# Column sums of V's weights moved from TensorE to VectorE, four raw blocks, and a re-paired set of first loads

## The chip, the cores and the metric

The kernel runs on one core of one Trainium2 chip. The metric is the device time of one execution in microseconds (us). A core has five engines with a program each: TensorE (PE in the profile, PEld for its weight loads), VectorE (DVE), ScalarE (ACT), GpSimd (POOL) and SyncE (SP). DMA transfers are issued from the queues of SP, ACT and POOL, which the profile calls SPq, ACTq and POOLq.

## The reference

```python
xn  = layernorm(x)                                  # x: 2048 x 512, no scale or shift
# A: local dilated attention, 32 heads of 16, window of 8 keys two rows apart
q, k, v = split(xn @ wqkv)                          # wqkv: 512 x 1536
o   = softmax(q . k[s - 2w], w = 0..7) weighted sum of v[s - 2w]
A   = o @ wo
# B: gated MLP
z   = gelu(xn @ w_in)                               # w_in: 512 x 1792, halves z1, z2
g   = w_sp @ layernorm(z2) + b_sp                   # w_sp: 2048 x 2048
B   = (z1 * g) @ w_out                              # w_out: 896 x 512
out = x + A + B
```

Everything is bfloat16 with float32 accumulation.

## The kernel before

The 2048 rows are handled as 16 blocks of 128 rows (index b), and as 4 waves of 512 rows (index j or tc). The program is not written in its final order. Each step is a task with an engine, inputs, outputs, an estimated duration and a priority. A planner (`Plan.schedule`) places the tasks in time by these estimates, gives out the eight PSUM banks, and so fixes the order of instructions on every engine and every DMA queue; the hardware then runs each engine's list strictly in that order and waits on semaphores. For the first microseconds part of the order is written by hand: lists of task names that must follow one another (`for names in (...)`), and a table `land` of the moments at which the planner is to believe the first loads landed.

The tasks that the change and the prediction touch, with their lines in the profile of before:

- Loads. `ldx0` (L541) and `ldx1` go out on ACT's queue; `ldwv0`, `ldwv1` (V's weights in two halves, L518), `ldx2`, the two halves `ldwin2a` (L524) and `ldwin2b` (L530) of z2's weights, `ldx3` to `ldx7` (L514), `ldq` and `ldk` (L536) and `ldx8` to `ldx15` go out on SP's queue, in this order.
- `ln_block(b)`: `bnst` and `bnag` take mean and variance on DVE (L599, L601), `vpe` adds epsilon (L609), POOL takes the power -1/2 (`rstd`, L611), DVE normalises (`norm`, L623). The normalised block is then turned, so that features lie on partitions: blocks 0 to 3 by four small PE matmuls (`xTr`, L579) and an ACT copy (`xTe`, L587), blocks 4 to 15 by a DMA transpose on SP's queue (`xTd`, L617).
- Raw blocks. V of blocks 0 and 1 does not wait for the normalisation. PE turns the raw x (`xTx`, L579), ACT copies it (`xTc`, L606), PE multiplies it with V's weights (`V0`, `V1`, L654), and the mean is taken out afterwards: `cs_0` and `cs_1` (L638) multiply a matrix of ones with V's weights, which puts minus the column sums on every partition (`cse`, L642), `fix0` and `fix1` (L660, DVE) add mean times column sum, and `Ve0`, `Ve1` (L663, ACT) scale by `rstd` and write the result. From block 2 on V is computed from the turned normalised block, and `Ve` only copies. POOL's queue writes every V block to DRAM (`Vw`, L668).
- PE's main work, in the order of the program: z2 = gelu(...) in blocks (`z2_b`, L766, eviction L774, squares L779), Q and K in pairs per wave (`Q0_0`, `K0_0`, ..., L677, eviction `QKe` L686), z1 (L812), the big product g with `w_sp` (L907), and the output blocks `outo_b` and `out_b` (L963, L972).
- DVE's main work: the products of Q and shifted K (`prod`, `padd`, L698 and L703), the softmax steps (L728 to L752), normalisation of z2 (`zn`, L798), the weighted sums of V per block (`pv`, `pva`, `pvb`, `pvc`, L935 to L941), the gating (`gb`, `u`, L918 and L921) and the last addition of every output block (`fin_b`, L978). `red0` and `red2` (L713) are small PE steps that sum the products over a head; `red2` stands in the middle of g and needs `padd3_3`, the last of the products.
- Output blocks use PSUM banks in turn: until block 5 they alternate between two banks, so `outo4` needs `fin2` and `outo9` needs `fin7`.

Of the kernel before, what the change touches and what calls it, by code (L numbers as in the profile page):

```python
# [36 lines left out]
class Plan:  # L37
# [85 lines left out]
    def schedule(self, dma_bw=300.0, xbar_bw=190.0, dma_lat=1300.0, dma_pre=400.0, issue=None, tol=40.0, land=None,  # L123
# [49 lines left out]
        while left:  # L173
            pick = None
            for e in ENGS:
                sc = []
                for t in cand[e]:
                    r = max(t.ready, free[e])
                    for b in t.banks:
                        if b.base is None:  # L180
                            p = place(b)
                            if p is None:
                                r = None
                                break
                            r = max(r, p[2])
# [31 lines left out]
            if t.dma is not None:  # L217
                iss = issue[e]
                t.eng_end = r + iss
# [4 lines left out]
                t.end = xe + dma_lat  # L224
# [114 lines left out]
def build_kernel(nc, A_x, A_wqkv, A_wo, B_x, B_w_in, B_w_sp, B_b_sp, B_w_out, out, report=False, emit=True):  # L339
# [11 lines left out]
    NXT = 4  # L351
    NWARM = 8
# [3 lines left out]
    vscr = nc.dram_tensor("vscr", (16 + S, 512), BF).ap()  # L356

# [13 lines left out]
    place(3584, w_in1=0, tg=0, On=2048, xcT=0, ncs=1024)  # L371
# [8 lines left out]
    off["xn"] = off["attn"]  # L380
    AR = top[0]
# [4 lines left out]
    for name, n in (("prime", 4), ("mx", 128), ("Zb", 256), ("Z", 128), ("maskt", 128), ("st6", NB * 6),  # L386
                    ("mv", NB * 2), ("vpe", NB), ("rstd", NB), ("s1", NB), ("s2", NB), ("m2", NB), ("msq", NB),
# [8 lines left out]
    with ExitStack() as es:  # L396
# [57 lines left out]
        R1(("wqk", 0), "wqk", 2048)  # L454
        R1(("wqk", 1), "wqk", 2048, 2048)
        for s_ in range(2):
            R1(("wv", s_), "wv", 1024, 1024 * s_)
# [8 lines left out]
        for hf in range(2):  # L466
            for b in range(2):
                R1(("xcT", b, hf), "xcT", 256, 512 * b + 256 * hf)
            R(("xnT", 0, hf), "sb", [(off["xnT"] + dc * S, off["xnT"] + dc * S + 128) for dc in (2 * hf, 2 * hf + 1)])
        R1("ncs", "ncs", 1024)  # L470
# [20 lines left out]
        def dma(eng, fn, nbytes, chan, reads=(), writes=(), name="", xbar=False, prio=0.0, after=()):  # L491
            return T(eng, fn, reads=reads, writes=writes, name=name, prio=prio, after=after,
                     dma=dict(chan=chan, nbytes=nbytes, xbar=xbar))
# [7 lines left out]
        ncs = A("ncs", 1024).bitcast(F32)  # L501
# [15 lines left out]
        def ld_wv(hf):  # L517
            dma("sp", lambda e: e.dma_start(AC(off["wv"] + 1024 * hf, [[512, 2], [1, 512]]),  # L518
                                            A_wqkv[256 * hf:256 * hf + 256, 1024:1536].rearrange("(c p) n -> p c n",
                                                                                               p=128)),  # L520
                256 * 512 * 2, ("wv", hf), writes=[("wv", hf)], name="ldwv%d" % hf)
# [13 lines left out]
        def ld_wqk(which, eng):  # L535
            dma(eng, lambda e: e.dma_start(  # L536
                AC(off["wqk"] + 2048 * which, [[512, 4], [1, 512]]),
                A_wqkv[:, 512 * which: 512 * which + 512].rearrange("(c p) n -> p c n", p=128)),
                512 * 512 * 2, ("wqk", which), writes=[("wqk", which)], name="ld%s" % ("qk"[which]))

        dma("act", lambda e: e.dma_start(A("xin", 512), x2[0:128, :]), 128 * 512 * 2, ("xin", 0),  # L541
            writes=[("xin0", 0), ("xin0", 1)], name="ldx0")
        ld_x(1, "act")
        ld_wv(0)
        ld_wv(1)
        ld_x(2, "sp")
        ld_win2a()
        ld_win2b()
        ld_x(3, "sp")
        ld_x(4, "sp")  # L550
        ld_x(5, "sp")
        ld_x(6, "sp")
        ld_x(7, "sp")
        ld_wqk(0, "sp")
        ld_wqk(1, "sp")

# [16 lines left out]
        def pe_tr(src, keys, name):  # L573
# [8 lines left out]
            T("pe", tr, reads=keys + ["ident"], writes=[bk], est=(430.0 if name == "xTx0" else 4 * c_mm(128)), name=name)  # L582
# [10 lines left out]
        def ln_block(b):  # L593
# [9 lines left out]
            if b < 2:  # L603
                bc = pe_tr(xin, xk, "xTx%d" % b)
                for hf in range(2):
                    T("act", (lambda hf: lambda a: a.activation(A("xcT", 256, 512 * b + 256 * hf), P(bc, 256, 256 * hf),  # L606
                                                                ACTF.Copy))(hf),
                      reads=[bc], writes=[("xcT", b, hf)], est=c_act(256), name="xTc%d_%d" % (b, hf), prio=-1)
# [23 lines left out]
        def colsum():  # L632
            bk = plan.bank("cs")
            for hf in range(2):
                def mm(t, hf=hf):
                    last = None
# [433 lines left out]
```

## Time and profile before

| | us |
|---|---|
| three executions | 236.80, 237.02, 237.28 |
| median | 237.02 |
| span of the profiled execution, first to last instruction | 236.1 |
| what lies around the span, against the median | 0.9 |
| PE busy in the span | 231.7 |
| DVE busy | 207.4 |
| ACT busy | 96.5 |
| POOL busy | 32.7 |
| granted TensorE clock, mean | 1.000 |

Busy time of an engine is the union of its instructions; a matmul is counted to the end of its drain, so a busy PE says that matmuls follow one another, not that each is at its peak. The start of one 128x512 matmul follows the one before by 0.216 us, that of a 128x448 one by 0.189 us, and four 128x128 ones take 0.224 us from the first start to the next group, although the profile's durations for them are 0.379, 0.352 and 0.219 us.

### The profile page before, as it was taken

Reading aid. Unit: us, or ns where it says so; the run is one execution under the profiler, and the core shown is the slowest. Engines: PE = TensorE matmul, PEld = TensorE weight load, DVE = VectorE, ACT = ScalarE, POOL = GpSimd, SP = SyncE. Lnnn points to the kernel's source line nnn. Section 1 sums busy time; section 2 is a strip of 40 time slices with the busy share of each in tenths; the row PEclk is TensorE's granted clock in tenths of the full one; section 3 lists DMA queues with packets and bytes.
Section 4 is the critical chain, followed back from the end, with each engine's and each line's share of the span. In section 5 each row is a group of like instructions: output and inputs, shape, how many; then the busy total and the mean of one; then the engine's idle time right before and its main releaser. Section 6 shows DMA issues by size and latency. Waiting matters only on the chain.

```text
span 236.1 us, 2974 instructions
## 1 busy us (share of the span) xinstructions
PE 231.7 (98%) x1114; PEld 109.1 (46%) x1135; DVE 207.4 (88%) x269; ACT 96.5 (41%) x145; POOL 32.7 (14%) x56
## 2 busy tenths in 40 slices
PE   8999999999999999999999999999999999999996
PEld 3455555555444444444444444444444444444443
DVE  3799899999998899999699998986989997999432
ACT  3598889888967895510120531111111111000000
POOL 2259650311733100000000000000000000000000
PEclk9999999999999999999999999999999999999999
DMA  7998969991048325430999999998995959936432
GB/s 211 352 283 163 243 146 217 195 202 44 22 165 260 92 85 69 104 118 0 226 347 252 225 266 180 200 304 187 346 258 175 261 161 303 193 95 181 135 96 69
DMA packets 82013, 43.86 MB, mean 186 GB/s; under 512 B 54336, under 2 KB 81360, under 8 KB 82000
## 3 DMA queue, kind: packets, MB, share of 16 engines
q1 hardware_dynamic: 80768, 41.27, 71.5%
q0 software_dynamic: 800, 2.11, 2.8%
q10 hardware_dynamic: 432, 0.30, 0.6%
q8 instruction: 9, 0.15, 0.3%
q14 instruction: 4, 0.03, 0.1%
HBM read 26.35 MB, written 4.21 MB: 129 GB/s over the span
## 4 chain that ended last, share of the span: by engine, by line
PE 94%; DMA 3%; SPq 1%; ACT 1%; issue 1%; DVE 0%
PE ps L907 41%; PE ps L677 12%; PE ps L972 10%; PE ps L812 10%; PE ps L766 9%; PE ps L963 6%; PE ps L654 5%; DMA arena<-in_B_w_in_dram 3%; PE ps L713 1%; ACT arena L774 0%; SPq L518 0%; ACT arena L587 0%; PE ps L579 0%; SPq L514 0%; SPq L524 0%
## 5 line engine op out<-in xcount | busy, mean ns | idle before, releaser
L907 PE MATMUL ps<-arena 128*128 128x512 bf16 x439 | 96.6, 379 | 0.5
L907 PEld LDWEIGHTS ps<-arena 128*128 128x128 bf16 x448 | 43.7, 98 | 53.1 <-issue 0.4
L915 ACT ACTIVATE arena<-ps 128x1024 bf16<-128x1024 f32 (+1 forms) x16 | 14.7, 917 | 78.0 <-PE ps L907 78.0
L698 DVE TENSOR_TENSOR arena<-arena 128x4096 bf16<-128x4096 bf16 x16 | 36.5, 2282 | 0.1
L935 DVE TENSOR_TENSOR arena<-arena 128x4096 bf16<-128x4096 bf16 x16 | 36.4, 2283 | 0.0
L938 DVE TENSOR_TENSOR arena<-arena 128x2048 bf16<-128x2048 bf16 (+1 forms) x32 | 29.9, 948 | 0.0
L677 PE MATMUL ps<-arena 128*128 128x512 bf16 x126 | 28.7, 379 | 0.1
L703 DVE TENSOR_TENSOR arena<-arena 128x4096 bf16<-128x4096 bf16 x12 | 27.4, 2287 | 0.1
L972 PE MATMUL ps<-arena 128*128 128x512 bf16 (+2 forms) x117 | 26.9, 366 | 0.1
L766 PE MATMUL ps<-arena 128*128 128x448 bf16 x128 | 26.0, 352 | 0.5 <-DMA arena<-in_B_w_in_dram 0.5
L812 PE MATMUL ps<-arena 128*128 128x512 bf16 x110 | 24.4, 379 | 0.1
L978 DVE TENSOR_TENSOR arena<-ps,arena 128x512 bf16<-128x512 f32 (+2 forms) x17 | 11.2, 658 | 11.7 <-PE ps L972 11.7
L677 PEld LDWEIGHTS ps<-arena 128*128 128x128 bf16 x128 | 14.5, 113 | 13.0
L766 PEld LDWEIGHTS ps<-arena 128*128 128x128 bf16 x128 | 12.3, 98 | 12.7 <-ACT arena L642 0.7
L686 ACT ACTIVATE arena<-ps 128x1024 bf16<-128x1024 f32 x16 | 16.3, 1021 | 4.4 <-PE ps L677 4.1
L972 PEld LDWEIGHTS ps<-arena 128*128 128x128 bf16 x119 | 11.4, 98 | 12.8
L812 PEld LDWEIGHTS ps<-arena 128*128 128x128 bf16 x112 | 10.9, 98 | 13.2 <-ACT arena L818 0.3
L963 PE MATMUL ps<-arena 128*128 128x512 bf16 (+2 forms) x66 | 16.5, 366 | 0.1
L774 ACT ACTIVATE arena<-ps 128x896 bf16<-128x896 f32 x16 | 14.6, 914 | 3.2 <-PE ps L766 3.1
L818 ACT ACTIVATE arena<-ps 128x1024 bf16<-128x1024 f32 (+1 forms) x16 | 13.9, 923 | 4.9 <-PE ps L812 4.8
L654 PE MATMUL ps<-arena 128*128 128x512 bf16 x60 | 15.6, 379 | 0.2
L779 ACT ACTIVATE arena<-arena 128x896 bf16<-128x896 bf16 x16 | 15.1, 945 | 0.0
(61 smaller groups left out, 168.5 us busy)
## 6 DMA issues: line engine op xcount, KB each, us to landing
arena<-vscr SPq DMA_DIRECT2D x16, 1024.0 KB, 7.1
arena<-in_A_x_dram SPq DMA_DIRECT2D x30, 128.0 KB, 3.6
vscr<-arena POOLq DMA_DIRECT2D x16, 128.0 KB, 3.0
out_dram<-arena SPq DMA_DIRECT2D x15, 128.0 KB, 1.8
arena<-in_A_wqkv_dram SPq DMA_DIRECT2D x2, 512.0 KB, 6.9
arena<-in_B_w_in_dram SPq DMA_DIRECT2D x2, 448.0 KB, 6.1
arena<-in_B_w_in_dram SPq DMA_DIRECT2D x1, 896.0 KB, 5.9
arena<-in_B_w_out_dram SPq DMA_DIRECT2D x1, 896.0 KB, 4.9
```

What stands on the lines that cost most here:

```text
L654: last = t.matmul(P(bk, 512), A("xcT", 128, 512 * b + 128 * dc) if b < 2 else xTv(b, dc), A("wv", 512, 512 * dc), start=(dc == 0), stop=(d ...
L677: last = t.matmul(P(bk, 512, 512 * which), AC(off["wqk"] + 2048 * which + 512 * dc + c, [[4, 128]]), AC(off["xnT"] + dc * S + 512 * j, [[1 ...
L686: T("act", lambda a: a.activation(AC(qo, [[ko - qo, 2], [1, 512]]), P(bk, 1024).rearrange("p (t n) -> p t n", t=2), ACTF.Copy, scale=0.5), ...
L698: T("dve", (lambda pbv, qb, kb: lambda v: v.tensor_tensor(pbv, qb, kb, ALU.mult))(pbv, qb, kb), reads=rd, writes=[("pb", s_)], est=c_tt(40 ...
L703: T("dve", (lambda av, bv: lambda v: v.tensor_tensor(av, av, bv, ALU.add))(av, bv), reads=[("pb", 1)], writes=[("pb", acc)], est=c_tt(4096 ...
L766: last = t.matmul(P(bk, 448, 512 * hf), xTv(b, dc), AC(off["w_in2"] + 896 * dc + 448 * hf, [[1, 448]]), start=(dc == 0), stop=(dc == 3))
L812: last = t.matmul(P(bk, 512, 512 * i), AC(off["w_in1"] + 896 * dc + 128 * fc, [[1, 128]]), AC(off["xnT"] + dc * S + 512 * j, [[1, 512]]), ...
L907: last = t.matmul(P(bk, 512, 512 * i), AC(off["z2"] + FH * sh + 128 * fc, [[1, 128]]), AC(off["wT%d" % r_] + sh * 512, [[1, 512]]), start= ...
L935: T("dve", lambda v: v.tensor_tensor(tv, tv, av, ALU.mult), reads=[("attn", b)], writes=[("Vs", sv)], est=c_tt(4096), name="pv%d" % b, pri ...
L938: T("dve", (lambda n: lambda v: v.tensor_tensor(A("Vs", n, 4096 * sv), A("Vs", n, 4096 * sv), A("Vs", n, 4096 * sv + n), ALU.add))(n), wri ...
L963: last = t.matmul(P(bk, cn), AC(off["OT"] + 512 * tb + 128 * cc, [[1, 128]]), AC(off["wo"] + 512 * cc + c0, [[1, cn]]), start=(cc == 0), s ...
L972: last = t.matmul(P(bk, cn), AC(off["z1T"] + fc * S + 128 * tb, [[1, 128]]), AC(off["w_out"] + 512 * fc + c0, [[1, cn]]), start=False, sto ...
```

## The change

- `cs_0`, `cs_1` and `cse` are gone. V's weights are turned by four DMA transposes on SP's queue (`wvT0` to `wvT3`, L655 of the new file), behind `xTd11`; DVE sums them with one `tensor_reduce` over 128x4x512 elements (`csum`, L659); POOL's queue writes the 512 sums to DRAM (`csw`) and reads them back onto all partitions (`csr`).
- The raw way of computing V holds for blocks 0 to 3 (`NRAW = 4`). PE turns raw x2 and x3 too (`xTx2`, `xTx3`). The product is scaled by `rstd` into SBUF as float32, for blocks 0 and 1 by DVE (`Ve0`, `Ve1`), for 2 and 3 by ACT; later DVE adds the mean's part in SBUF (`fix0` to `fix3`, after `prod1_1`) with `mr`, minus mean times `rstd`.
- Block 3's normalised copy is turned by DMA (`xTd3`; `NXT = 3`), not by PE.
- x0 is loaded in two halves of 64 rows, one from SP's and one from ACT's queue; x2 with x3, x4 with x5 and x6 with x7 are loaded in pairs, x2 and x3 ahead of z2's weights. Q's and K's weights are one transfer of 1 MB from ACT's queue, behind ACT's copy `xTc2_0`. SP's queue issues `xTd3` between x4 and x6, ahead of x6 to x15. z1's weights (`ldwin1`) go behind `xTd15`, where they stood behind `xTd7`.
- One of the eight warm-up matmuls, a short one, is gone. The planner's figures for DMA transposes, its landing table and the hand-written order are new. On PE, V0 to V3 now all stand ahead of the first z2 block; on DVE, `pv1` moves from ahead of `padd3_3` to behind it, and in the last gating wave `u4_3` and `pvc12` stand between `fin1` and `fin2`, where they stood ahead of `fin1`.

```diff
-    NXT = 4
-    NWARM = 8
+    NXT = 3
+    NRAW = 4
+    NWARM = 7
...
+        for h, q_ in enumerate(("sp", "act")):
+            dma(q_, (lambda h: lambda e: e.dma_start(ar[64 * h:64 * h + 64, off["xin"]:off["xin"] + 512],
+                                                     x2[64 * h:64 * h + 64, :]))(h),
+                64 * 512 * 2, ("xin0", h), writes=[("xin0", h)], name="ldx0%s" % "ab"[h])
         ld_x(1, "act")
-        ld_wv(0)
-        ld_wv(1)
-        ld_x(2, "sp")
+        for d0, dn in ((0, 2), (2, 2)):
+            ld_wv(d0, dn)
+        ld_x2(2)
         ld_win2a()
         ld_win2b()
-        ld_x(3, "sp")
...
-        ld_wqk(0, "sp")
-        ld_wqk(1, "sp")
+        ld_x2(4)
+        ld_x2(6)
+        ld_wqk("act")
...
         def colsum():
-            bk = plan.bank("cs")
-            for hf in range(2):
-                def mm(t, hf=hf):
...
-            T("act", lambda a: a.activation(ncs, P(bk, 512), ACTF.Copy, scale=-1.0), reads=[bk],
-              writes=["ncs"], est=c_act(512), name="cse", prio=-0.5)
+            for dc in range(4):
+                dma("sp", (lambda dc: lambda e: e.dma_start_transpose(AC(off["wvT"] + 128 * dc, [[512, 4], [1, 128]]),
+                                                                      A("wv", 512, 512 * dc)))(dc),
+                    128 * 512 * 2, ("wvT", dc), reads=[("wv", dc)], writes=[("wvT", dc)], name="wvT%d" % dc, xbar=True,
+                    prio=0.5, after=lnd[4:12])
+            T("dve", lambda v: v.tensor_reduce(Fv("cs", 4), AC(off["wvT"], [[512, 4], [1, 512]]), AX.X, ALU.add),
+              reads=[("wvT", dc) for dc in range(4)], writes=["cs"], est=2290, name="csum", prio=4.5)
+            dma("pool", lambda e: e.dma_start(bass.AP(tensor=cscr.tensor, offset=cscr.offset, ap=[[4, 128], [1, 4]]),
+                                              Fv("cs", 4)),
+                2048, "cswr", reads=["cs"], writes=["cscr"], name="csw", prio=1)
+            dma("pool", lambda e: e.dma_start(csb, bass.AP(tensor=cscr.tensor, offset=cscr.offset, ap=[[0, 128], [1, 512]])),
+                128 * 2048, "csrd", reads=["cscr"], writes=["csb"], name="csr", prio=1)
...
         def v_block(b):
-            if b < 2:
-                T("dve", lambda v: v.scalar_tensor_tensor(P(bk, 512), ncs, Fv("mv", 1, 2 * b), P(bk, 512),
-                                                          ALU.mult, ALU.add),
-                  reads=["ncs", ("mv", b)], writes=[bk], est=690, name="fix%d" % b, prio=1)
...
+            if b < NRAW:
+                if b < 2:
+                    T("dve", lambda v: v.tensor_scalar(vraw(b), P(bk, 512), Fv("rstd", 1, b), None, ALU.mult),
+                      reads=[bk, ("rstd", b)], writes=[("vraw", b)], est=680, name="Ve%d" % b, prio=4)
+                else:
+                    T("act", lambda a: a.activation(vraw(b), P(bk, 512), ACTF.Copy, scale=Fv("rstd", 1, b)),
+                      reads=[bk, ("rstd", b)], writes=[("vraw", b)], est=c_act(512), name="Ve%d" % b, prio=4)
+                T("dve", lambda v: v.scalar_tensor_tensor(
+                    vdh.rearrange("p d (c h) -> p d c h", c=4), csb.rearrange("p (h d c) -> p d c h", d=16, c=4), Fv("mr", 1, b),
+                    vraw(b).rearrange("p (c h d) -> p d c h", d=16, c=4), ALU.mult, ALU.add),
+                  reads=["csb", "mr", ("vraw", b)], writes=[("Vn", sl)], est=690, name="fix%d" % b, prio=6)
...
-                      ["xTx0", "cs_0", "V0_0", "xTx1", "cs_1", "V0_1", "xTr0", "V1_0", "xTr1", "V1_1",
-                       "z2_0_0", "z2_0_0b", "z2_0_1", "xTr2", "z2_1_0", "z2_1_1", "V2_0", "V2_1", "xTr3", "z2_2_0"],
+                      ["xTx0", "xTx1", "V0_0", "V0_1", "V1_0", "V1_1", "V0_2", "xTx2", "V0_3", "V1_2", "V1_3", "xTx3", "V2_0", "V2_2",
+                       "xTr0", "V3_0", "V3_2", "xTr1", "z2_0_0", "z2_0_0b", "z2_0_1", "xTr2", "z2_1_0", "z2_1_1", "z2_2_0"],
...
+                      ("ldx4", "xTd3", "ldx6"), *[("xTd3", "ldx%d" % b) for b in range(8, NB)], ("V10_2", "Q3_3")):
```

## The prediction

> **What bounds the kernel now.** I read the page first, then the chain of waits in order of time, then the timelines of PE, SP's queue and DVE around the change.
>
> ```profile
> span 236.1 us, 2974 instructions
> PE 231.7 (98%) x1114; PEld 109.1 (46%) x1135; DVE 207.4 (88%) x269; ACT 96.5 (41%) x145; POOL 32.7 (14%) x56
> PE 94%; DMA 3%; SPq 1%; ACT 1%; issue 1%; DVE 0%
> ```
>
> PE carries 94% of the chain that ended last; the one other piece of any size is a DMA, 3% of 236. The chain in order of time says which:
>
> ```profile
> 2.79 6.50 DMA arena<-in_B_w_in_dram
> 9.34 0.93 PE ps L766 x4
> ...
> 15.47 6.47 PE ps L677 x30
> ```
>
> That is `ldwin2b`, z2's second half of weights. From 9.34 to the end PE hardly waits (its timeline; columns: start, length, what, then idle time before it):
>
> ```profile
> 7.34 0.59 PE L654 MATMUL ps<-arena 128*128 128x512 bf16 x2
> 8.22 0.92 PE L766 MATMUL ps<-arena 128*128 128x448 bf16 x4 [0.28 <-DMA arena<-in_B_w_in_dram]
> 9.34 0.93 PE L766 MATMUL ps<-arena 128*128 128x448 bf16 x4 [0.21 <-DMA arena<-in_B_w_in_dram]
> ...
> 15.31 1.03 PE L677 MATMUL ps<-arena 128*128 128x512 bf16 x4
> ```
>
> So the time is PE's list plus what PE waits for before Q0_0 (first L677, 15.31). By starts, PE lost 0.45 us before 8.22 (last V matmul 7.56 + 0.216 = 7.78) and 0.37 before 9.34 (8.785 + 0.189 = 8.97). What the change gains must be gained before Q0_0; behind it PE has the same matmuls.
>
> **PE's list up to Q0_0.** Gone: four 128x512 of `cs`, 4 x 0.216 = 0.86; `xTr3` for one more raw turn net, +0.22; one short warm-up, 0.11. V2 and V3 (8 x 0.216 = 1.73) move from behind the z2 wait to ahead of it. The new list from V0_0 on is V0 to V3, five turns (`xTx2`, `xTx3`, `xTr0` to `xTr2`) and three z2 blocks: 16 x 0.216 + 5 x 0.224 + 24 x 0.189 = 3.46 + 1.12 + 4.54 = 9.11 us.
>
> When V0_0 can start: x0 landed at 3.69 (bnst0 at 3.71), `xTx0` at 3.73, its ACT copy 4.38, V0_0 at 4.95 behind `cs_0`. Without `cs_0` it is ready at about 4.8 with x0 unchanged; with x0 as the head of two queues (half the bytes ahead of it) at 4.6, since the shorter warm-up ends at 3.46. I take 4.7. Waits inside the stretch: `xTx2` needs x2 and x3. In FIFO order 1.05 MB stand up to x3; the rate from 3 to 12 us was 356 GB/s with 190 KB moved before 3, so they are through by 5.4, landing 0.7 (as x2 did) to 1.7 us (as the later loads did) behind: 6.1 to 7.1. PE gets there at about 6.0. V1 waits for two ACT copies of 0.33 each. Together 0.1 to 1.3; I take 0.3, by x2's own row, the nearest. Q0_0: 4.7 + 9.11 + 0.3 = 14.1, against 15.31: -1.2 us.
>
> [...]
>
> z2's weights: 131 KB (x3) more stand ahead of them, 131 / 356 = 0.4 us: `ldwin2a` 8.09 to 8.5, `ldwin2b` 9.30 to 9.7. PE reaches them at 14.1 - 4.76 = 9.35 and 10.1. This wait, the chain's DMA piece, is hidden; next late are the inputs of Q0_0.
>
> **Inputs of Q0_0.** (a) Q's and K's weights, 1 MB at once, issued on ACT behind `xTc2_0`, at about 7.3. 3.28 MB then stand up to its end, moved by 11.7 at 356 GB/s; landing 1.7 behind (x7, `ldq` and `ldk` all landed 1.7 to 1.8 behind their bytes): 13.4. In time by 0.7. ACT's issue costs 0.45 us (as on ACTq before), ahead of `xTc3_0`; V3 has that much room.
>
> (b) `xTd3`. DVE's chain to `norm3`: bnst2 at 6.2, then bnst 0.69, bnag 0.18, vpe 0.15, norm 0.41, a second round and `Ve0` 0.69: ready at 9.8. Its landing is bounded by DMA transposes of the same size:
>
> ```profile
> 14.49 5.63 SPq L617 DMA_TRANSPOSE arena<-arena x4
> ...
> DMA to landing us min/median/max: 2.4/4.3/5.9
> ```
>
> The first, issued at 14.49 behind eight loads, took 4.9, landing 2.4 behind the last of these loads (17.04); the last, on an empty queue, 2.4. Here x4 and x5 are ahead (landing about 11) and the 1 MB runs beside it: 12.2 to 15.7, and 2.4 behind x5 gives 13.4, the nearest row. I take 13.5 and no wait; the late end costs 1.6.
>
> **The queues passed.** SP issues x6 to x15 only behind `xTd3`, so `xTd4` starts near 15.5 instead of 14.49, and x7 lands at about 14, not 11.25; bnst6 then waits, but Q1 needs `xTd7` only at 24 (25.2 before). The four `wvT` (1.31 each) push `xTd12` to `xTd15` by 5.2 us, `ldwin1` to a landing of about 42 (26.2 before; z1 starts at 73.35) and the `w_sp` transposes by 6 (g starts at 98.39). Covered by 30 us or more. POOL holds `csw` and `csr` ahead of `zr1` and `Vw4`; two transfers at 3.0 (as L668) end some 8 us behind `csum`, `fix0` is 17 us of DVE work behind it. `Vw0` to `Vw3` are read from 97.66 on.
>
> **DVE.** Added before `red2`: `csum` 2.4 (twice the 1.21 us of L728, which reduces half as many elements; 1.2 if bfloat16 ran at double rate), four fixes for two (2 x 0.75 by L660; float32 from SBUF with short strides, 0.4 to 1.5 each), `Ve0` and `Ve1` 2 x 0.61: +5.1. Moved behind `padd3_3`: pv1 and its sums, 2.20 + 1.14 + 0.60 + 0.33 = 4.3. Net +0.8.
>
> ```profile
> 113.30 0.69 DVE L918 TENSOR_TENSOR arena<-arena 128x1024 bf16<-128x1024 bf16 x1 [1.01 <-ACT arena L915]
> 113.91 2.28 DVE L703 TENSOR_TENSOR arena<-arena 128x4096 bf16<-128x4096 bf16 x1
> ...
> 117.31 1.05 PE L713 MATMUL ps<-arena 128*32 128x512 bf16 x16
> ```
>
> `padd3_3` ended at 116.19, 1.1 ahead of `red2`, behind a wait of 1.01 for PE. With DVE +0.8 and PE -1.2 the wait is used up and a spare of 0.3 stays; the earlier waits in this stretch (0.52, 0.70, 0.59) lie at steps that now stand later and give back up to 1.8. I take no stall; `csum`, should `wvT3` land after DVE reaches it (32.3 to 34.8 against 34.4), adds at most 0.5 (behind it stand `zn0` and the next products; behind `fix0` stands `padd1_1`).
>
> The tail has one loss:
>
> ```profile
> 200.95 0.69 DVE L978 TENSOR_TENSOR arena<-ps,arena 128x512 bf16<-128x512 f32 x1 [0.41 <-PE ps L972]
> 201.56 0.41 DVE L921 TENSOR_TENSOR arena<-arena 128x512 bf16<-128x512 bf16 x1
> 201.89 2.29 DVE L935 TENSOR_TENSOR arena<-arena 128x4096 bf16<-128x4096 bf16 x1
> 204.10 0.68 DVE L978 TENSOR_TENSOR arena<-ps,arena 128x512 bf16<-128x512 f32 x1
> ...
> 205.50 1.03 PE L963 MATMUL ps<-arena 128*128 128x512 bf16 x4
> ```
>
> `fin1` waits for PE; `fin2` follows 3.15 later and ends at 204.78, 0.72 before `outo4`, which needs its bank. Now `u4_3` (0.60) and `pvc12` (0.33) stand between: 0.94 - 0.72 + about 0.1 for the semaphore = 0.3 us that PE waits. `fin7` and `outo9` move by the same and hold.
>
> **Sum.** -1.2 + 0.3 = -0.9. The span goes from 236.1 to 235.2, and with the 0.9 around it the time from 237.0 to 236.1.
>
> **Rivals.**
> 1. Q0_0 waits (for `xTd3` beside the 1 MB, or for the 1 MB itself). For: 12.2 to 15.7 straddles 14.1. Against: the nearest row gives 13.4. At 14.9 it eats 0.8: 236.9, no change.
> 2. DVE becomes the bound, slower than before. Place: `red2`, then `fin2`. DVE has little idle time left from 26 to 160. Price: if the strided fixes cost 1.5 each (+3.0) or `csr` comes late, `padd3_3` is 3.0 later, less the spare of 0.3 and about 1.2 of the waits given back: `red2` holds PE 1.5 and the sum is +0.6: 237.6. It decides once DVE is 2.5 us later than I count. Against: L660 reads the same number of elements in 0.75.
> 3. The clock rises later. In the trace the first `cs` matmul starts follow by 0.40 us (4.26, 4.66), those from 4.95 on by 0.216. The granted clock of the first microsecond slices reads 1.00 and does not show it; the starts do. The new list has gaps of about 0.5 us between 3.9 and 4.7, where before PE ran on. [...]
> 4. The change does less than it says: x0's halves and the pairs land later than taken, V starts at 5.2, Q0_0 at 14.6: 236.6.
>
> **How the numbers follow.** A measurement here can tell about 0.2%, 0.5 us, from no change. Forecast 0.48 (almost all faster), rival 1 0.20 (three quarters same), rival 2 0.16 (two thirds slower), rival 3 0.07 (slower), rival 4 0.09 (half faster, half same). Faster 0.53, same 0.27, slower 0.20. The low end is Q0_0 at 13.9 and no loss at `outo4`: 235.6; the high end stops between rivals 1 and 2 at 237.5, which leaves out rival 3 and the worse half of rival 2. The forecast's own range is 235.6 to 236.5.
>
> **What would show it.** Right: first L718 (Q0_0) near 14.1, no DMA wait at z2, a wait of some 0.3 at `outo4`, none at `red2`. Wrong: a wait of the first Q on a DMA; PE waiting on DVE at the 32x512 matmuls in g; V matmuls that follow by 0.4 after 5 us; the fixes far over 0.75.

## The result, and the profile after

| | before | after |
|---|---|---|
| median, us | 236.91 (6 runs, 236.78 to 237.37) | 238.69 (6 runs, 237.72 to 239.90) |
| ratio after to before | | 1.0071, 95% interval 1.0047 to 1.0095 |
| span of the profiled execution, its time | 236.1, 237.28 | 237.0, 238.25 |
| PE busy, DVE busy | 231.7, 207.4 | 232.2, 212.5 |

The changed kernel is slower by 0.7%, 1.8 us; the forecast was 0.9 faster. Its runs also spread over 2.2 us where those of before spread over 0.6 (1.1 to 1.4 in the larger sets timed with the experiments, beside one run at 239.51), and that turned out to be about half of the answer. First the page of the profile after, in the same three places as before:

```profile
span 237.0 us, 3003 instructions
PE 232.2 (98%) x1134; PEld 108.8 (46%) x1134; DVE 212.5 (90%) x275; ACT 95.4 (40%) x143; POOL 32.3 (14%) x58
PE 84%; DVE 10%; DMA 2%; ACT 1%; issue 1%; SPq 1%; DVEq 0%
```

PE's share of the chain that ended last fell from 94% to 84%, and DVE, which had none, has 10%. The DMA in that chain is no longer z2's weights but the load of x2 with x3:

```profile
2.56 4.54 DMA arena<-in_A_x_dram
...
15.35 6.91 PE ps L718 x32
```

PE's timeline around the change (L599 turns, L689 V, L807 z2, L718 Q and K):

```profile
3.46 0.58 PE L599 MATMUL ps<-arena 128*128 128x128 bf16 x4
4.99 0.40 PE L599 MATMUL ps<-arena 128*128 128x128 bf16 x4 [0.96 <-DMA arena<-in_A_x_dram]
5.23 1.63 PE L689 MATMUL ps<-arena 128*128 128x512 bf16 x5
7.14 0.40 PE L599 MATMUL ps<-arena 128*128 128x128 bf16 x4 [0.28 <-DMA arena<-in_A_x_dram]
...
10.42 1.68 PE L807 MATMUL ps<-arena 128*128 128x448 bf16 x8
...
15.19 2.10 PE L718 MATMUL ps<-arena 128*128 128x512 bf16 x9
```

The wait for z2's weights is gone, as forecast (the halves landed at 9.07 and 10.33, ahead of PE). Q0_0 starts at 15.19, not 14.1: PE stands still for x1 before `xTx1`, V0_0 begins at 5.23, and inside the V list it waits for the second half of V's weights (landed 6.43) and for x2 and x3 (7.10). `xTd3`, which the prediction bounded by 12.2 and 15.7, landed at 14.28:

```profile
10.88 1.29 SPq L638 DMA_TRANSPOSE arena<-arena  x1
...
DMA to landing us min/median/max: 2.4/2.4/4.3
```

DVE and PE at the middle of the kernel (fixes L702, `padd1_3` and `padd3_3` L744, `red0` and `red2` L754):

```profile
54.26 4.20 DVE L702 SCALAR_TENSOR_TENSOR arena<-arena,fpool 128x512 bf16<-128x512 f32 x4
69.24 2.28 DVE L744 TENSOR_TENSOR arena<-arena 128x4096 bf16<-128x4096 bf16 x1
71.58 1.05 PE L754 MATMUL ps<-arena 128*32 128x512 bf16 x16 [0.30 <-DVE arena L744]
114.15 2.29 DVE L744 TENSOR_TENSOR arena<-arena 128x4096 bf16<-128x4096 bf16 x1
117.56 1.05 PE L754 MATMUL ps<-arena 128*32 128x512 bf16 x16
```

`red2` has no wait, as forecast; `red0`, 46 us earlier, has one that the prediction did not look for. In the kernel before, `padd1_3` (L703) ended at 63.19, 1.4 ahead of `red0` (L713):

```profile
60.90 2.29 DVE L703 TENSOR_TENSOR arena<-arena 128x4096 bf16<-128x4096 bf16 x1
64.64 1.05 PE L713 MATMUL ps<-arena 128*32 128x512 bf16 x16
```

The fixes cost 1.1 each, not 0.75. And the tail (`fin1`, `pvc12`, `fin2` on DVE; `outo4` on PE):

```profile
201.26 0.69 DVE L1020 TENSOR_TENSOR arena<-ps,arena 128x512 bf16<-128x512 f32 x1 [0.75 <-PE ps L1014]
202.47 0.42 DVE L983 TENSOR_TENSOR arena<-arena 128x512 bf16<-128x512 bf16 x1
205.34 0.69 DVE L1020 TENSOR_TENSOR arena<-ps,arena 128x512 bf16<-128x512 f32 x1
206.17 1.02 PE L1005 MATMUL ps<-arena 128*128 128x512 bf16 x4 [0.27 <-DVE arena L1020]
```

In this pair of traces Q0_0 gained 0.12, `red0` lost 0.37 and `outo4` 0.43 by the starts of the matmuls (the brackets show idle time, which is counted from the end of the matmul before and so is less); the last DVE instruction ends 0.67 later. The profiled execution of after lies 0.4 under its own median, so a part of the loss is not in this trace.

### The profile page after: what moved, and what is told of

It is laid out like the page before. It is cut to its first block, busy times and chain, and to the rows that moved or that the text cites. A ratio compares the mean times of both kernels' runs of the same rounds, so it can differ in the third digit from the quotient of the medians.

```text
span 237.0 us, 3003 instructions
## 1 busy us (share of the span) xinstructions
PE 232.2 (98%) x1134; PEld 108.8 (46%) x1134; DVE 212.5 (90%) x275; ACT 95.4 (40%) x143; POOL 32.3 (14%) x58
## 4 chain that ended last, share of the span: by engine, by line
PE 84%; DVE 10%; DMA 2%; ACT 1%; issue 1%; SPq 1%; DVEq 0%
PE ps L949 41%; PE ps L853 10%; PE ps L1014 9%; PE ps L718 9%; PE ps L807 7%; PE ps L1005 5%; DVE arena L739 3%; DVE arena L744 3%; DMA arena<-in_A_x_dram 2%; PE ps L689 2%; DVE arena L702 2%; DVE arena L839 1%; DVE arena L1020 1%; PE ps L754 1%; ACT arena L815 1%
## 5 line engine op out<-in xcount | busy, mean ns | idle before, releaser
L718 PE MATMUL ps<-arena 128*128 128x512 bf16 x128 | 28.9, 379 | 0.0
L744 DVE TENSOR_TENSOR arena<-arena 128x4096 bf16<-128x4096 bf16 x12 | 27.4, 2284 | 0.1
L807 PE MATMUL ps<-arena 128*128 128x448 bf16 x128 | 25.7, 352 | 0.0
L718 PEld LDWEIGHTS ps<-arena 128*128 128x128 bf16 x128 | 14.5, 113 | 13.0
L807 PEld LDWEIGHTS ps<-arena 128*128 128x128 bf16 x128 | 12.4, 98 | 11.6 <-ACT arena L700 0.2
L689 PE MATMUL ps<-arena 128*128 128x512 bf16 x64 | 16.1, 379 | 0.0
L815 ACT ACTIVATE arena<-ps 128x896 bf16<-128x896 f32 x16 | 14.6, 918 | 3.2 <-PE ps L807 3.2
```

The lines of the kernel that those rows point to most:

```text
L689: last = t.matmul(P(bk, 512), A("xcT", 128, 512 * b + 128 * dc) if b < NRAW else xTv(b, dc), A("wv", 512, 512 * dc), start=(dc == 0), stop ...
L718: last = t.matmul(P(bk, 512, 512 * which), AC(off["wqk"] + 1024 * dc + 512 * which + c, [[4, 128]]), AC(off["xnT"] + dc * S + 512 * j, [[1 ...
L744: T("dve", (lambda av, bv: lambda v: v.tensor_tensor(av, av, bv, ALU.add))(av, bv), reads=[("pb", 1)], writes=[("pb", acc)], est=c_tt(4096 ...
L807: last = t.matmul(P(bk, 448, 512 * hf), xTv(b, dc), AC(off["w_in2"] + 896 * dc + 448 * hf, [[1, 448]]), start=(dc == 0), stop=(dc == 3))
L815: T("act", lambda a: a.activation(A("z2", FH, FH * b).rearrange("p (t n) -> p t n", t=2), PC(bk.col(), [[512, 2], [1, 448]]), ACTF.Gelu_ap ...
```

## The experiments

The kernels below carry short labels (e1 to i2), by which the expectations name one another. All have their order of instructions written out, so that an edit moves nothing else. Each ratio is to the kernel before, timed on the same chip in the same rounds.

**The changed kernel again (e1).** No edit beside the written-out order.

> The changed kernel with its order of instructions written out instead of planned, otherwise the same: the base for the next three. Two theories of where the predicted 1.2 us and more went. DVE: the added work on VectorE (column sums 2.28, four fixes of 1.11 instead of 0.75 each) makes it late for red0 (PE waited 0.37 there) and for fin2 (0.43 before outo4). Loads: halves and pairs made the first loads slow (x1 landed 4.95, second half of wv 6.43, x2 with x3 7.10), so that V0_0 began at 5.23 and Q0_0 at 15.19, and runs differ by 2 us where those of before differ by 0.6. Both expect 238.7 here, 1.007 of the kernel before; a second trace should show Q0_0, red0 and outo4 within 0.3 us of the first one's, else they are not what the whole difference is made of.

Measured: 238.82 (237.83 to 240.97), ratio 1.0079 (1.0048 to 1.0110). It is the changed kernel, spread and all. In its trace Q0_0 starts at 14.82, not 15.19, but PE waits 0.85 at `outo4`, not 0.27: the same three places, with other sizes in each run.

**x0 in one transfer (e2).**

```diff
-        for h, q_ in enumerate(("sp", "act")):
-            dma(q_, (lambda h: lambda e: e.dma_start(ar[64 * h:64 * h + 64, off["xin"]:off["xin"] + 512],
-                                                     x2[64 * h:64 * h + 64, :]))(h),
-                64 * 512 * 2, ("xin0", h), writes=[("xin0", h)], name="ldx0%s" % "ab"[h])
+        dma("act", lambda e: e.dma_start(A("xin", 512), x2[0:128, :]), 128 * 512 * 2, ("xin", 0),
+            writes=[("xin0", 0), ("xin0", 1)], name="ldx0")
```

> x0 in one transfer from ACT's queue as before, everything else as in the changed kernel. Loads: SP's and ACT's heads are as before, so x0 lands at 3.7, x1 at 4.6, wv's halves at 4.2 and 5.3; V0_0 starts near 4.9 instead of 5.23, Q0_0 near 14.8, the time is 0.3 to 0.5 under the changed kernel's (238.3), and the runs lie within 1 us. DVE: x0 0.5 later changes nothing that counts, Q0_0 stays near 15.2, 238.7.

Measured: 237.80 (237.21 to 238.48), ratio 1.0028 (1.0006 to 1.0049): 1.2 us by the ratios, more than either theory gave (0.3 to 2.1 by the intervals), and the runs lie within 1.3 us. V0_0 starts at 4.81 and z2 at 9.42, a full 1.0 earlier than in the first trace; yet Q0_0 starts only at 14.94, because `xTd3` lands at 14.85. So the prediction's rival 1 appears as soon as PE is on time.

**The tail of VectorE's list as before (e4).**

```diff
-fin0_0 gb4_3 gb6_3 fin1_0 u4_3 pvc12 u6_3 pv13 fin2_0
+fin0_0 gb4_3 u4_3 gb6_3 pvc12 fin1_0 u6_3 pv13 fin2_0
```

> In the tail of VectorE's list alone, u4_3 and pvc12 stand ahead of fin1 again (fin0 gb4_3 u4_3 gb6_3 pvc12 fin1 u6_3 pv13 fin2), as before. The wait of PE at outo4 (0.43 in the changed kernel's trace) goes, unless u6_3 and pv13 end late for another reason: 238.25 by either theory, if the prediction's term for the tail (0.3) was right; 238.7 if pva12 or gb6_3 then hold fin2 instead.

Measured: 239.15 (237.77 to 240.89), ratio 1.0087 (1.0055 to 1.0119). In the trace the wait at `outo4` is gone (`fin2` ends at 205.03, `outo4` starts at 205.53), but the time does not show it; the traced run, 237.77, is the fastest of its ten. Something else moves the runs by more than this.

**One part of the change alone: the kernel before with x0 in halves (f1).** The edit is the reverse of that of x0 in one transfer, made to the kernel before.

> The kernel before, its order written out, with one part of the change alone: x0 in two halves, the first at the head of SP's queue, the second of ACT's. Loads: each issue behind it is 0.5 to 0.6 later on SP, wv's halves land 0.4 to 1 later than the 4.22 and 5.32 of before and z2's second half 0.5 to 0.8 later than 9.30; z2 waits for that half in this kernel, so Q0_0 goes from 15.3 to 15.8 or 16.1; 237.6 to 238.0, with runs 2 us apart instead of 0.6 to 1.2. DVE: x0 lands 0.4 to 0.7 earlier, the rest is as before; 237.0 with the runs as close as before.

Measured: 238.67 (237.91 to 238.86), ratio 1.0058 (1.0041 to 1.0075). The halves landed at 3.06 and 3.31 (the whole at 3.69), and everything behind them later: x1 5.23 for 4.59, V's weights 4.74 and 5.82 for 4.22 and 5.32, z2's 9.20 and 10.44 for 8.09 and 9.30. The first z2 matmuls in PE's timeline of this kernel (L876):

```profile
9.24 0.93 PE L876 MATMUL ps<-arena 128*128 128x448 bf16 x4 [0.81 <-DMA arena<-in_B_w_in_dram]
10.49 0.93 PE L876 MATMUL ps<-arena 128*128 128x448 bf16 x4 [0.32 <-DMA arena<-in_B_w_in_dram]
```

In the kernel before, 8.22 and 9.34. This part alone costs 1.4 us there, through z2's weights (Q0_0 comes at 16.45, 1.1 later).

**x0 in one transfer and the tail as before (f2).**

> The changed kernel with x0 in one transfer and the tail of VectorE's list as before (both undone). x0 in one transfer alone gave 237.8, with PE waiting 0.2 at outo4 in its trace (0.8 and 0.4 in traces of the changed kernel); with the tail 237.3 to 237.6 by both theories, no wait at outo4, and 0.37 of wait at red0 left. If the tail is worth nothing: 237.8.

Measured: 237.57 (237.23 to 239.51), ratio 1.0034 (1.0017 to 1.0051). The profiled run is the longest, 239.51, and its DVE timeline shows what a long tail looks like (L1089 is `pvc12`, L1126 `fin1`):

```profile
203.08 0.43 DVE L1089 TENSOR_TENSOR arena<-arena 128x512 bf16<-128x512 bf16 x1 [1.96 <-DMA arena<-arena]
203.43 0.68 DVE L1126 TENSOR_TENSOR arena<-ps,arena 128x512 bf16<-128x512 f32 x1
```

`pvc12` writes the half of On that the transpose `OTd10` still reads. `OTd10` was issued at 198.58 and landed at 203.06, 4.5 us later; in the other traces of this order it took 2.4 (200.82 in the kernel with the tail alone), 3.9 (f4, below) or 4.5 (202.77 in the changed kernel again). In the kernel before `pvc10` ends 7.8 us ahead of `pvc12`; the change's order leaves 3.8 or less. In this run PE then waits twice, 0.77 at `outo3` and 0.51 at `outo4`.

**Without the chain of column sums (f3).** As f2, and without `wvT`, `csum`, `csw`, `csr`, `mr` and the fixes; `Ve0` to `Ve3` write V at once.

> As f2, and without the chain of column sums (no DMA transposes of wv, no sum, no csw and csr, no fixes; V of blocks 0 to 3 is written without its mean term). DVE: the 7.5 us that this takes off VectorE ahead of red0 remove the wait there, so PE's start sets the end: 0.3 to 0.5 under f2, near 237.0. Loads: red0's wait is small beside Q0_0; Q0_0 stays at 14.9 (xTd3 holds it) and the time at 237.3 to 237.5; DVE's work is then paid by idle time.

Measured: 237.41 (236.58 to 240.57), ratio 1.0021 (0.9997 to 1.0044), against 1.0034 with the chain. `padd1_3` ends at 68.40 instead of 71.39, and the wait at `red0` is gone: `red0` starts at 70.88 instead of 71.53, the first z1 matmul at 73.60 instead of 74.25. So DVE's added work does cost about 0.6 in the trace, but runs above 238 are still there: the spread is not DVE's.

**Block 3 turned on TensorE again (f4).** Made to f2.

```diff
-    NXT = 3
+    NXT = 4
...
-z2_1_1 z2_2_0
+z2_1_1 xTr3 z2_2_0
```

> As f2, with block 3 turned on TensorE and copied by ACT as before (five turns become six) instead of by DMA. xTd3 landed at 14.85 with x0 in one transfer and PE waited 0.6 for it. Loads: Q0_0 comes at 14.3 to 14.5 and the time falls by 0.4 to 0.5 against f2, to 236.9. DVE: red0 is held by VectorE's chain (wvT3, csum, fixes, products), which does not start earlier by it; Q0_0 earlier only makes the wait at red0 longer (0.37 to 0.9), and the time is that of f2, unless the transposes of wv come earlier too because SP no longer waits for norm3.

Measured: 239.62 (238.54 to 239.84), ratio 1.0100 (1.0081 to 1.0118): 1.6 us worse, as neither theory had it. SP no longer waits for `norm3`, so x6 to x15 go out from 3.9 us on (from 12.22 in the changed kernel), and the 1 MB of Q's and K's weights lands at 15.98 (13.68 there); Q0_0 starts at 16.26. `xTd3` in SP's queue also served as a gate that kept x6 to x15 behind most of that transfer; with them held back again, in h1, it lands at 12.97.

**Block 10's sum finished before `pv12` (g1 with x0 in one transfer, g4 with the halves).** On SP, `ldVs14` also moves ahead of `st0`.

```diff
-pvc11 pv10 pv12 pva10 pva12 pvb10 pvb12 pvc10 fin0_0 gb4_3 gb6_3 fin1_0 u4_3 pvc12 u6_3
+pvc11 pv10 pva10 pvb10 pvc10 pv12 pva12 pvb12 fin0_0 gb4_3 u4_3 gb6_3 pvc12 fin1_0 u6_3
```

> As f2, but block 10's sum on VectorE is finished before pv12 begins (pv10 pva10 pvb10 pvc10 pv12 pva12 pvb12), and on SP ldVs14 stands ahead of st0. New theory, from f2's trace, which caught one of its long runs (239.51): pvc12 writes the half of On that the DMA transpose OTd10 still reads. In the changed kernel's list pvc10 ends some 4 us before pvc12 (7.8 in the kernel before), and OTd10 takes 2.4 us on some runs and 4.5 on others; on those VectorE stops for 0.7 to 2.0, fin1 and fin2 come late and PE waits twice (0.77 and 0.51). With pvc10 3.8 us earlier the long runs go: all runs between 237.0 and 237.8, median 237.4. Rival: the runs differ by their first loads; then 237.2 to 239.5 as in f2.

> The changed kernel with its loads untouched (x0 in halves) and only VectorE's and SP's tail as in g1. By the theory of On's halves its runs, 237.8 to 241.0 in the changed kernel, come down to between 237.3 and 238.6, median 238.0; what is left above g1 (0.6) is what x0's halves cost. If the halves make the spread, the median stays at 238.5 or more with runs over 240.

Measured for g1: 237.82 (237.11 to 239.52), ratio 1.0044 (1.0026 to 1.0063); for g4: 239.59 (237.88 to 240.12), ratio 1.0096 (1.0070 to 1.0122). In both traces `OTd10` lands 3 us ahead of `pvc12` and the tail has no wait, and yet the long runs remain: On's halves explain the long tail of one trace, not the spread. The second trace, of a run of 240.12, shows two other things, x1 that lands late and a half rate that lasts. PE's timeline (L707 turns, L797 V):

```profile
5.73 0.61 PE L707 MATMUL ps<-arena 128*128 128x128 bf16 x4 [1.64 <-DMA arena<-in_A_x_dram]
6.13 2.34 PE L797 MATMUL ps<-arena 128*128 128x512 bf16 x5
8.27 0.63 PE L707 MATMUL ps<-arena 128*128 128x128 bf16 x4
```

The same five V matmuls and four turns take 1.63 and 0.40 in the trace of after. Here V's matmuls follow by 0.43 until 10.2 us, by 0.216 from then on. From V0_0 to z2 the list takes 6.37 (6.13 to 12.50), against 4.36 of work without the waits in after: 2.0 us for a full rate that comes late, of which the waits of after would have hidden 0.8. Q0_0 starts at 17.26, 2.07 later than in after: 0.90 of it is there at V0_0 already (x1 landed at 5.69, not 4.95), the rest is the list's. The first matmul at full rate, by starts, with the profiled runs' own times:

| kernel | `xTx1` starts | full rate from | Q0_0 | time |
|---|---|---|---|---|
| after | 4.99 | 4.99 or earlier | 15.19 | 238.25 |
| e1 | 4.22 | 6.6 | 14.82 | 238.55 |
| g2 (below) | 4.79 | 9.0 | 16.21 | 238.59 |
| g4 | 5.73 | 10.2 | 17.26 | 240.12 |

**`red0` behind V15 (g2).** Made to g1.

```diff
-V13_2 red0 V14_0 V14_2 V15_0 V15_2 z1_0_0
+V13_2 V14_0 V14_2 V15_0 V15_2 red0 z1_0_0
```

> As g1, and red0 behind V15 on TensorE (8 V matmuls, 1.73 us, between), so that PE has other work while VectorE finishes padd1_3. DVE: the wait at red0 (0.30 to 0.41 by the traces) goes and z1 starts that much earlier: 237.0. Rival: VectorE's next steps behind red0 (smask, smax0) come later and red2 then holds PE, 237.4 as g1.

Measured: 237.25 (236.48 to 239.27), ratio 1.0024 (1.0002 to 1.0046), against 1.0044 without. No wait at `red0`, none at `red2`; the long runs remain, and this profile (238.59) is one of them, with the half rate up to 9.0 us.

**Matmuls on constants in PE's first gaps (g3 on g2; h2 on the changed kernel).**

```diff
-    NWARM = 7
+    NWARM = 9
...
+        for wi in range(4):
+            T("pe", lambda t: t.matmul(P(bw, 128), ones[:, 0:128], ones[:, 0:128], start=True, stop=True),
+              writes=[bw], est=107.0, name="fill%d" % wi, prio=1000)
```

> As g2, with six matmuls of 128 columns on constants put in the gaps of PE's first 5 us: two behind the warm-up, four between xTx0 and xTx1. In the traces with x0 in one transfer V0's matmuls followed each other by 0.43 up to 6.6 us in two of them (f2, f3) and by 0.22 from 4.8 or 5.5 on in two others: a late clock, worth 0.4 to 0.9 us. If the gaps (0.30 and 0.65) are the reason, the full rate is there from about 5 us as in the kernel before, and the time is 236.4 to 236.8. If not, 237.0 as g2 or 0.1 more.

> The changed kernel, loads, fixes and tail untouched, with eleven matmuls of 128 columns on constants between xTx0 and xTx1 alone (PE idles there 0.3 to 1.9 us in the traces of kernels with x0 in halves). Clock theory: long runs of the changed kernel are those in which the first V matmuls follow by 0.43 instead of 0.22 for long (up to 10.2 us in g4's trace, 240.12). Without the gap the full rate is there by 7 us at the latest: median 237.9 to 238.2 instead of 238.8, no run above 239.2. Rival (the loads alone make it long): median 238.5 to 239.0, runs up to 240.9 as before.

Measured for g3 (four such matmuls between `xTx0` and `xTx1`): 237.28 (236.70 to 237.91), ratio 1.0011 (1.0000 to 1.0023); the runs above 238 are gone, the median is that of the kernel without. Measured for h2, the changed kernel with eleven of them there and nothing else: 238.09 (237.92 to 238.27), ratio 1.0042 (1.0026 to 1.0058). Its runs lie within 0.35 us, where they lay within 3.1. In its trace (L712 turns, L694 the constants, L802 V) the full rate is there early, and V0_0 now waits for V's weights without losing it:

```profile
3.89 0.83 PE L694 MATMUL ps<-const-bfloat16-1.0 128*128 128x128 bf16 x11
4.56 0.38 PE L712 MATMUL ps<-arena 128*128 128x128 bf16 x4
5.93 1.24 PE L802 MATMUL ps<-arena 128*128 128x512 bf16 x5 [0.99 <-DMA arena<-in_A_wqkv_dram]
```

That is what the clock theory expected, and its rival, the loads alone, did not. Of the 34 runs of the four kernels with the same first loads and no constants (after, e1, e4, g4) 24 took more than 238.4; of h2's six none did. The short runs stay: h2's trace has Q0_0 at 15.25 and its run took 238.24, the first trace of the changed kernel 15.19 and 238.25. So the constants take away the long runs, which are worth 0.9 us on the mean by the ratios of e1 and h2 (0.1 to 1.7 by their intervals). That they do so through the rate rests on the traces: full rate came between about 3.9 and 6.7 us in the five traces with constants, and at 9.0 and 10.2 in two of the ten with this first list and without.

**What still holds Q0_0 (h1, i1).** In g3's trace z2's work ends near 14.1 and PE waits; first PE's timeline, then the stretches of 1 us with PE's busy time, its clock, the DMA share and GB/s:

```profile
15.14 2.13 PE L828 MATMUL ps<-arena 128*128 128x512 bf16 x9 [0.90 <-DMA arena<-arena]
```

```profile
11.00:12.00 1.00, 1.00 (x10) 1.00 2.10 271
12.00:13.00 1.00, 1.00 (x7) 1.00 2.00 67
```

From 12 to 14 us the engines moved almost nothing (25 GB/s in the next stretch), while `xTd3` (issued 9.63, landed 15.09) and the last of the 1 MB (landed 14.39) were both under way. In g1's trace `xTd3`, issued at 9.76, landed at 13.00 and the 1 MB at 12.42. In every trace `xTd3` lands 0.5 to 0.7 behind the 1 MB, from 13.0 to 15.4. The kernel h1 is g3 without `xTd3`, but with its gate (x6 to x15 wait for `bnst4`); i1 is h1 with eight constants instead of four:

```diff
-    NXT = 3
+    NXT = 4
...
+        byname["ldx6"].deps.add(byname["bnst4"])
```

> As g3, with block 3 turned on TensorE and copied by ACT instead of by DMA, and SP's loads of x6 to x15 held behind bnst4 (in f4 they were not held, the 1 MB of Q's and K's weights landed at 15.98 and Q0_0 began at 16.26). In g3's trace z2's work ended near 14.1 and PE waited about 1 us for xTd3, landed 15.09; between 12 and 14 us the DMA moved only 67 and 25 GB/s while 256-byte packets of that transpose and the last 2048-byte packets of the 1 MB took their time. Theory (transpose and the 1 MB hold each other up): without xTd3 the 1 MB lands by 13.5, Q0_0 starts at 14.3 to 14.5, and the time falls by 0.6 to 0.8 against g3, to 236.5. Rival (the 1 MB is late by itself): it lands at 14.4 as in g3 and the time is 237.0 or more.

Measured for h1: 237.18 (236.62 to 237.74), ratio 1.0001 (0.9988 to 1.0014). The 1 MB lands at 12.97 (x6 at 13.92), and z2 runs into Q0_0 with 0.22 of idle time between by the profile; the first recorded Q matmul starts at 14.84, and three Q records are missing. From issue to landing the 1 MB took 6.3 us here and 5.7 in i1, with no transpose beside it, and 5.3 to 7.9 in the twelve traces with one (5.5 in g1, 7.9 in g3), in six of them no longer than here. So it was slow only beside a transpose, and not always there; that the two hold each other up is likely, not shown. The trace of h1 is 0.63 shorter than that of before (span 235.43), but that run is among the fastest of its kernel and the one of before among the slowest; by the medians nothing is won.

> As h1 with eight matmuls on constants instead of four between xTx0 and xTx1. h1's trace has the full rate from 3.8 us and Q0_0 near 14.45, its span 0.6 under that of the kernel before, but 7 of its 12 runs lie 0.5 to 1.0 above the 5 fastest. If that is the late clock again (its gap ahead of xTx1 was still 0.4), eight close it: all runs within 0.7 us, median 236.6, faster than before by 0.15% to 0.2%. If it is the loads, 237.2 as h1.

Measured for i1: 237.81 (237.18 to 238.59), ratio 1.0021 (1.0007 to 1.0035): worse. In its trace x1 landed at 5.19 instead of 4.62 and V0_0 started at 5.63, with the full rate from about 5.9. Four more constants did not bring the rate forward here; the late x1 is what differs in the trace. What spreads the runs of h1 and i1 (1.1 and 1.4 us) stays open; those of before spread over 1.2 and 1.4 in the same rounds.

**Where the halves cost (h3, i2).** First both halves on ACT's queue in the kernel before, then the changed kernel with its halves and three repairs (eleven constants, the tail, `red0` behind V15).

> The kernel before with x0 in two halves, both at the head of ACT's queue, so that SP's queue is as before. With one half on each queue (f1) wv, x2 and z2's weights were issued 0.62 to 0.76 later and landed 0.5 to 1.1 later, and the time rose by 1.4. If the half at the head of SP's queue is what costs (its issue, 0.59, stands ahead of eight loads), z2's second half lands near 9.3 again and the time is 237.0 to 237.3. If it is the smaller transfers themselves (203 and 176 GB/s from 2.5 to 3.5 us against 266 and 381), it is 237.7 to 238.5 still.

> The changed kernel with x0's halves kept and three repairs: h2's eleven matmuls on constants, g1's tail, g2's place for red0. h2 took 238.09 with 0.43 of wait at red0 in its trace and fin2 at 205.59; the two waits are worth 0.4 and 0.4 by the traces: 237.3 to 237.5, and what is left above g3 (237.28, the same with x0 in one transfer) is the halves' own price once the clock is up in time: 0 to 0.2. If the halves cost by late loads and not through the clock, 238.0 or more.

Measured for h3: 239.92 (238.76 to 240.30), ratio 1.0109 (1.0086 to 1.0133), and for i2 237.53 (236.85 to 237.87), ratio 1.0011 (1.0001 to 1.0021). On ACT's queue alone the halves landed at 4.26 and 5.42, and x1 behind them at 7.23 (4.59 before), while SP's loads came as before (`ldwin2b` 9.42). Each half took about as long as a whole transfer (1.16 between them; 0.90 between x0 and x1 in the kernel before), PE began at 5.56 and ran at half rate until 10.1, and Q0_0 came 2.7 later than before, at 17.98. So the halves can cost without an issue at the head of SP's queue and without late loads behind it. But it is another loss than f1's: here x0 itself is whole only at 5.42, there x0 came early and z2's weights late.

The kernel i2 stands where the same kernel with x0 in one transfer stands (g3; both 1.0011, timed in different rounds). That the halves cost through the clock alone, as the expectation has it, is not shown by this. In i2's trace (L802 V, L712 turns) the eleven constants themselves run at half rate, V0_0 begins at it, and the full rate comes only at 6.7:

```profile
5.60 1.70 PE L802 MATMUL ps<-arena 128*128 128x512 bf16 x5
7.14 0.39 PE L712 MATMUL ps<-arena 128*128 128x128 bf16 x4
```

PE loses nothing by it, since the turn at 7.14 needs x2 with x3, which landed at 7.07 (7.16 in h2, where the turn starts at 7.21). And in both i2 and g3 Q0_0 waits for `xTd3` (15.43 and 15.09), which hides part of what comes late ahead of it.

Nor is the gap in front of x1 always there. In four of the seven traces with a half on each queue (after, e4, f1, g4) ACT's issue of x1 takes 0.85 and x1 lands at 4.91 to 5.69, V's first weights at 4.56 to 5.30; in the three others (e1, h2, i2) it takes 0.59, x1 lands at 3.73 to 4.18 and V's first weights at 4.92 to 5.79. V0_0 needs both, and starts at 5.06 to 6.13 in the six that have the new list. What sets which comes first, and how much of the spread of the runs it makes, no run tests.

## Why the prediction was wrong

By the ratios (times 237 us) the difference of 1.9 between the changed kernel and before falls to 1.0 with the constants (0.9 for the clock) and to 0.3 with `red0` and the tail repaired (0.7 for DVE, 0.3 to 1.2 by the intervals). The rest, from 0.3 down to the forecast's -0.9, is the gain at Q0_0 that did not come: in i2's trace Q0_0 starts at 15.56, 0.25 later than before, where -1.2 was forecast. Step by step:

- **V0_0 at 4.7: the step that failed first.** It was worked out from x0 alone. In the new list `xTx1` stands ahead of V0_0, so V0_0 waits for x1, which landed at 4.95 behind two halves; V0_0 came at 5.23, and at 4.8 to 5.6 with x0 in one transfer. The mechanism expected of the halves, an earlier x0, was there (3.01 and 3.27, the whole at 3.69 in the kernel before), but the step did not ask what stands behind them. Both on one queue, the halves landed one behind the other (4.26 and 5.42, h3); one on each queue, both landed ahead of the whole. What decided stood behind them, x1 or V's first weights.
- **Waits of 0.3 inside the list: mis-sized.** By the starts in the trace of after, 0.21 for the ACT copies of x1, 0.16 for the second half of V's weights and 0.45 for x2 with x3: 0.8. With the 0.5 of V0_0 that is all of the 1.1 by which Q0_0 missed 14.1 in this trace; the 9.11 of work were right.
- **The clock: rival 3, given 0.07, came true in part of the runs, and is about half of the slowdown.** The prediction had its sign. No run shown by then gives its price; 2.0 was measured in the worst trace (g4). The gaps of about 0.5 that it counted were taken from the landings of before; with the halves the gap ahead of `xTx1` was 0.3 to 1.8 us. The same first list had full rate at 5.5 or earlier in e2 and at 9.0 in g2, and over the traces of nearly this list the moment lay between about 3.9 and 10.2 us; what sets it within that range is not shown. Why the kernel before was hurt less is argued, not shown: PE waits 0.45 and 0.37 there for z2's weights, and a late clock would eat those waits first. The change removed this cover, and the prediction counted the waits as gain without asking what else they hid. No trace of the kernel before with a late clock was taken, and one of its runs, at 239.51, was long too.
- **z2's weights hidden: right,** at 9.07 and 10.33 instead of 8.5 and 9.7.
- **`xTd3` at 13.5 and no wait: late, and no wait by luck.** It landed at 14.28, behind the forecast's Q0_0, and between 13.0 and 15.4 in all traces, always behind the 1 MB. In the changed kernel PE is late enough not to notice; with PE on time it waits 0.6 in e2 and 0.9 in g3, rival 1 at its price, and not in g1, where it landed at 13.00.
- **DVE: the sum was 5.1, it is 6.7.** `csum` 2.28 as taken; `Ve0` and `Ve1` 0.74 each, not 0.61; the fixes 4 x 1.1, within their bounds but far from the 0.75 taken by L660, the nearest row in elements but not in access pattern (here runs of 8 elements at strides of 16 and 64); `csum` waited 0.73 for `wvT3`. `csr` landed 14.3 us behind `csum`'s end, not 8, still ahead of `fix0`. The check was made at `red2`, which did hold. `red0` came first and was not looked at: 0.37. The 4.3 that the net of +0.8 takes off do not help there, since `pv1` stood behind `padd1_3` (at 104.52 in the kernel before); and the new list has four steps more, `zn8` to `zn11`, ahead of `padd1_3`, 1.6 us. That is rival 2 by kind, at another place and a quarter of its price.
- **The tail: right, but for one wait.** 0.3 was forecast; PE idled 0.18 to 0.27 at `outo4` in three traces with this tail (after, e2, h2) and 0.85 in e1, where `pvc12` also waits 0.65 for `OTd10`; the new order leaves `OTd10` 3.8 us or less between `pvc10` and `pvc12`. The kernels with that repaired alone did not show the gain in their medians, where the spread of the runs is larger; repaired together with `red0` it shows (1.0042 to 1.0011).
- **Rival 4** had V0_0 at 5.2 right, for a reason that is half right: the pair of x2 and x3 landed at the late end of what was taken, the halves of x0 did not. Q0_0 at 14.6 and 236.6 did not follow from it, since it left the waits behind V0_0 and the clock as they were.

What stays open: why the median of h1, the kernel with all repairs, only equals that of the kernel before (1.0001), when its one trace has Q0_0 0.5 earlier or more and a span 0.6 shorter; that trace is of one of its five fastest runs, and the slower ones were not traced. Open too is how the loss splits between the late clock and the late loads in a run that has both, as g4's has. That the granted clock is the cause of the half rate rests on the spacing of the matmuls and on the constants; the profile's own clock column reads 1.00 throughout.

## What to carry to other kernels

A wait that an edit removes may have been hiding something that varies from run to run: before counting it as gain, ask what else can come late in that stretch, here probably PE's full rate (from 10.2 us on in g4). Check every place where an engine's list is needed, the first above all: work that is saved behind it does not help there. When a transfer is moved ahead, follow the ones behind it to the step that needs them last, not the one that became earlier. And a spread of the runs that grows is a finding of its own: a single trace shows one draw, so look at the times of all runs before explaining the median by one profile, and try filling short gaps of PE at the start, which here took the long runs away (h2: 237.92 to 238.27).

## What the runs showed of the hardware

- PE ran at half rate (0.43 between 128x512 matmuls, 0.216 later) until about 3.9 to 10.2 us in executions of kernels with nearly the same first list (10.2 in g4, 9.0 in g2; about 3.9 to 6.7 with matmuls on constants in the first gap); a gap of 1.2 us after the rate had risen (4.72 to 5.93 in h2) did not bring it back down.
- A DMA of 64 rows took a queue about as long as one of 128: 1.16 us between two halves on one queue (h3; 0.90 between two whole ones in the kernel before), and an issue of 0.54 to 0.61 instead of 0.42 to 0.46 us (0.58 and 0.57 in the changed kernel).
- With a DMA transpose and the end of a 1 MB load both under way, the DMA engines moved 67 and 25 GB/s from 12 to 14 us in one execution (g3; 379 two us earlier) and 138 and 279 in another (g1). In all twelve traces with the two side by side the transpose landed 0.5 to 0.7 us behind the load (14.28 and 13.68 in the changed kernel).
- A DMA transpose of one block landed 2.4 to 4.5 us after its issue in the same place of the program (`OTd10`: 4.5 in f2 and e1, 3.9 in f4, 2.4 in e4).
- `scalar_tensor_tensor` over 512 float32 elements with inner runs of 8 strided elements took 1.1 us (L702 of the changed kernel), against 0.75 with contiguous operands, one of them in PSUM (L660 of the kernel before).
